# First four blocks' tap sums as diagonal matmuls, and another order of the first blocks

## The chip, the cores and the metric

The kernel runs on one core of one Trainium2 chip. A run's time is device microseconds of that core for one execution. Three runs of the kernel before gave 2386.4, 2385.7 and 2384.95 us, median 2385.7 us.

## The reference

`x` is 4 sequences of 4096 tokens with 192 channels. Each channel is first filtered along the tokens: seven taps, the softmax of a row of `weight` (8 rows, one for each 24 channels), zeros before the start. Then come two layers, the first with weights `moe_w_in`, `moe_w_out`, the second with `moe2_w_in`, `moe2_w_out`; these four are float64.

```
w = exp(weight - max); w = w / (sum(w) + 1e-09)
out = np.einsum('hk,bskhg->bshg', w, x_unf)      # 7 taps
h = x @ w_in                                     # [16384, 192] @ [192, 2048]
g = h * np.cos(h); x = g @ w_out                 # layer 1
h = np.maximum(x @ w_in, 0.0); out = h * h @ w_out   # layer 2
```

## The kernel before

**Tiling.** Channels lie on partitions, tokens on the free axis. The 16384 tokens make 32 blocks `n` of `T` = 512, the 2048 hidden units 16 chunks `c` of 128. An item is (layer `l`, block `n`, chunk `c`), with `l` = 0 for the first layer, 1 for the second. An item has products into `h` (the input side, "IN") and, after its elementwise chain, products into the two accumulators `o` of its block ("OUT"). Every float32 operand of TensorE is split into a rounded part and a rest, and three of the four part products are taken. All matmuls are 64 rows deep; a matmul on the lower 64 rows of the array and one on the upper 64 run as a pair. A step of the plan (a slot) takes IN of two items (18 matmuls) and OUT of two items (20): 19 pairs.

**The chain of an item.** Layer 0: `k` (L591, ScalarE), `f` (L603, VectorE), `sin` (L610, ScalarE), `g` (L617, VectorE), `hi` (L643, ScalarE), `lo` (L648, VectorE). Layer 1: `relu` (L627), `sq` (L636) and `hi`, all ScalarE, then `lo`. For some items of block 1 `lo` may go to GpSimd: 16 do. A bank of `h` is free again after `g` (layer 0) or `relu` (layer 1); there are four banks, two for a slot.

**Before the first layer.** For each block and each of two halves of its channels, `conv` loads `x`, makes the seven taps on VectorE (L375 once, L378 six times), and splits the sum into `xs` (L393, L397).

**Between the layers.** When a block's OUT is done, `ends` takes the sums out (L669, L679), adds the two halves (L698, L699, L723) and splits them into a new `xs` for layer 1 (L710, L715, L729, L734). There are four sets of `xs`.

**Weights.** `prep` loads a float64 weight unit (two chunks, seven DMAs on SyncE, L252 to L259), and makes float32 hi and lo parts of it: VectorE L270, L288, L302, L311, L326, L337 to L341, ScalarE L278, L332. There are 8 units for each layer.

**Two streams.** The items form two streams, `xs` and `ys`: the first holds (0,0), (0,2), (0,3) ... (0,31), (1,31), the second (0,1), (1,0), (1,1) ... (1,30), written (layer, block). A slot mostly takes one item of each. OUT follows IN by 3 slots in the first stream and 2 in the second (`LAGS`). An item that OUT takes alone ("single") is five matmuls in each of two turns, since both turns write the same banks.

**Order.** `Order.run` is a list scheduler with fixed costs: it writes every engine's instructions in one order, each with a due time from `start_of(slot)`. On the chip each engine goes through its list in that order and waits at the head.

Of the kernel before, what the change touches and what calls it, by code (L numbers as in the profile page):

```python
# [27 lines left out]
LEAD = 4  # L28
EARLY = 3
LAGS = (3, 2)  # L30
BUFS = {"raw": 2, "s": 2, "m": 2, "x": 3, "t": 12, "g": 11, "h": 4, "o": 4, "xs": 4}


PAIR, DRAIN, WAY = 233, 170, 90

# [11 lines left out]


def pool(n):
    return 200 + n * 2.4  # L50
# [17 lines left out]
class Order:  # L68
# [14 lines left out]
    def run(self):  # L83
        for s in self.steps:
            s.left = len(s.after)
            for a in s.after:
                a.next.append(s)
        ready = {}
        for s in self.steps:
            if not s.left:  # L90
                self.open(ready, s)
        clock = {}
        done = 0
        while done < len(self.steps):
            best = None
            for e, todo in ready.items():
                now = clock.get(e, 0.0)
                pick = None
                for s in todo:
                    if s.end is not None:  # L100
                        continue
                    at = max(now, s.ready)
                    for kind, n in s.takes:
                        have = self.free[kind]
                        if len(have) < n:
                            break
# [40 lines left out]
def tile_kernel(  # L147
# [10 lines left out]
    engines = {"V": V, "A": A, "G": G}  # L158
# [76 lines left out]
    OX = (HI + U - R, 0)  # L235
# [5 lines left out]
    tiles("m", [P, U], I32)  # L241

    def prep(l, u, due):
# [16 lines left out]

        a = order.add("load" + name, {"S": 400}, load, takes=(("raw", 1),), due=due - 12000, way=5000)
# [80 lines left out]

        return order.add("l" + name, {"V": two(U) + 300}, low, (h,), frees=((d, "m"),), due=due - 1500)


    tiles("x", [P, T + PAD], F32)
# [11 lines left out]
    def conv(n, due):  # L358

        own = order.add(f"x1.{n}", {"N": 0}, lambda s, e: None, takes=(("xs", 1),), due=due - 20000, way=0)  # L360
        last = []
        for j in (0, 1):
            d = due - (1 - j) * 6500

            def load(s, e, j=j):
                nc.sync.dma_start(s.got["x"][0], xp[:, n, j])

            a = order.add(f"x{n}.{j}", {"S": 100}, load, (own,), (("x", 1),), due=d - 12000, way=2500)
            y = b = None
            for k in range(K):  # L370

                def tap(s, e, a=a, y=y, k=k, j=j):
# [11 lines left out]
                    (a, taps) if k == 0 else (b,),  # L384
# [14 lines left out]
            b = order.add(f"xh{n}.{j}", {"A": act(T)} if n < EARLY else {"V": one(T)}, high, (b,), due=d - 1400)  # L399
# [3 lines left out]
        split[0, n] = own, last  # L403

# [113 lines left out]
    first = [(0, 0)] + [(0, n) for n in range(2, NB)] + [(1, NB - 1)]  # L518
    other = [(0, 1)] + [(1, n) for n in range(NB - 1)]
# [3 lines left out]

    slots = []
    x = y = 0
    late = len(xs) - NC
    pend = ([], [])
    while x < len(xs) or y < len(ys) or pend[0] or pend[1]:
        s = len(slots)
        ins = ()  # L530
        if x < LEAD:
            ins = (0, xs[x]), (0, xs[x + 1])
            x += 2
        elif x == late and y < late + LEAD:
            ins = (1, ys[y]), (1, ys[y + 1])
            y += 2
        elif x == late and pend[0]:
            pass
        elif x < len(xs) and y < len(ys):
            ins = (0, xs[x]), (1, ys[y])  # L540
            x, y = x + 1, y + 1
        elif x < len(xs):
            ins = (0, xs[x]), (0, xs[x + 1])
            x += 2
        for k, it in ins:
            pend[k].append(it)
            it.slot = s
        outs = []
# [3 lines left out]
        extra = []  # L552
        while pend[0] and pend[0][0].slot + LAGS[0] < s:
            extra.append(pend[0].pop(0))
        while pend[1] and pend[1][0].slot + LAGS[1] < s:
            extra.append(pend[1].pop(0))
        slots.append((tuple(it for _, it in ins), tuple(outs), tuple(extra)))

# [13 lines left out]
    for (l, u), s in preps.items():  # L572
        weights[l, u] = prep(l, u, start_of(s))
    for (l, n), s in blocks.items():
        if l == 0:
            conv(n, start_of(s))

    def chain(it):
# [44 lines left out]
        else:  # L623
# [23 lines left out]
            {"V": 685, "G": pool(T)} if it.slot < 18 and it.n == 1 else {"V": 685},  # L647
            lambda s, e: engines[e].tensor_tensor(  # L648
# [8 lines left out]
    def ends(it, done):  # L657
# [36 lines left out]
        if l == 0:  # L694
# [45 lines left out]
            if 0 < n < NB - 2:  # L740

                split[0, n + 2][0].after.append(own)
        else:
# [3 lines left out]
                {"S": 100},  # L747
# [21 lines left out]
                {"S": 100},  # L769
# [86 lines left out]
    for s, (ins, outs, extra) in enumerate(slots):  # L856
        for turn in (0, 1):
# [54 lines left out]
```

## Time and profile before

| what | value |
|---|---|
| span of the profiled execution | 2385.6 us |
| time of the profiled execution | 2387.46 us |
| median of three runs | 2385.7 us |
| TensorE busy, matmuls | 2312.1 us (97%), 19456 |
| VectorE busy | 1843.3 us (77%) |
| ScalarE busy | 1911.7 us (80%) |
| GpSimd busy | 30.0 us (1%) |
| mean granted TensorE clock | 0.991 |

The busy time of TensorE counts a matmul from start to modelled end, and two halves overlap, so how far TensorE is from being full is read from the number of matmuls that start in a stretch, not from the 97%.

### The profile page before, as it was taken

Reading aid. Unit: us, or ns where it says so; the run is one execution under the profiler, and the core shown is the slowest. Engines: PE = TensorE matmul, PEld = TensorE weight load, DVE = VectorE, ACT = ScalarE, POOL = GpSimd, SP = SyncE. Lnnn points to the kernel's source line nnn. Section 1 sums busy time; section 2 is a strip of 40 time slices with the busy share of each in tenths; the row PEclk is TensorE's granted clock in tenths of the full one; section 3 lists DMA queues with packets and bytes.
Section 4 is the critical chain, followed back from the end, with each engine's and each line's share of the span. In section 5 each row is a group of like instructions: output and inputs, shape, how many; then the busy total and the mean of one; then the engine's idle time right before and its main releaser. Section 6 shows DMA issues by size and latency. Waiting matters only on the chain.

```text
span 2385.6 us, 46741 instructions
## 1 busy us (share of the span) xinstructions
PE 2312.1 (97%) x19456; PEld 2253.4 (94%) x19456; DVE 1843.3 (77%) x3001; ACT 1911.7 (80%) x3278; POOL 30.0 (1%) x22
## 2 busy tenths in 40 slices
PE   3879999999999999999999999999999999999999
PEld 2668999999999999999999999999999999999988
DVE  8999788777888777788777788877788877778643
ACT  3677888888888888888888888888888888888865
POOL 0220000000000000000000000000000000000000
PEclk9989999999999999999999999999999999999999
DMA  3121000000000000000000000000000000000000
GB/s 106 54 59 40 17 17 17 17 6 12 17 17 17 17 12 6 17 17 17 17 13 5 17 17 17 17 17 3 15 17 17 17 17 8 10 17 8 8 8 14
DMA packets 30820, 45.14 MB, mean 19 GB/s; under 512 B 3984, under 2 KB 12176, under 8 KB 30608
## 3 DMA queue, kind: packets, MB, share of 16 engines
q1 hardware_dynamic: 30608, 42.16, 6.0%
q8 instruction: 152, 2.49, 0.4%
q14 instruction: 60, 0.49, 0.1%
HBM read 29.56 MB, written 12.58 MB: 18 GB/s over the span
## 4 chain that ended last, share of the span: by engine, by line
PE 93%; DVE 5%; SPq 1%; ACT 0%; issue 0%; DMA 0%; POOL 0%; DVEq 0%; ACTq 0%; POOLq 0%
PE o L411 49%; PE h L411 44%; DVE t L378 1%; DVE t L603 1%; DVE t L617 1%; DVE g L648 0%; DVE m L302 0%; DMA raw<-in_w_dram 0%; DVE s L311 0%; SPq L259 0%; DVE wt L337 0%; DVE m L326 0%; DVE s L270 0%; ACT t L591 0%; DVE m L288 0%
## 5 line engine op out<-in xcount | busy, mean ns | idle before, releaser
L411 PE MATMUL o<-g,wt 64*128 64x512 f32 x10240 | 1514.6, 394 | 5.5 <-DVE g L648 2.5
L411 PE MATMUL h<-xs,wt 64*128 64x512 f32 x9216 | 1400.1, 396 | 62.9 <-ACT xs L393 27.5
L411 PEld LDWEIGHTS o<-g,wt 64*128 64x128 f32 x10240 | 1224.5, 185 | 38.4 <-PE o L411 9.3
L411 PEld LDWEIGHTS h<-xs,wt 64*128 64x128 f32 x9216 | 1161.7, 186 | 88.2 <-ACT xs L393 28.0
L648 DVE TENSOR_TENSOR g<-t,g 128x512 fp32r<-128x512 f32 x1008 | 689.0, 684 | 57.1 <-PE o L411 28.2
L643 ACT CAST g<-t 128x512 fp32r<-128x512 f32 x1024 | 625.7, 614 | 116.7 <-DVE t L617 115.5
L603 DVE TENSOR_TENSOR t<-h,t 128x512 f32<-128x512 f32 x512 | 351.3, 687 | 340.8 <-ACT t L591 340.6
L591 ACT ACTIVATE t<-h,quarter 128x512 int32<-128x512 f32 x512 | 350.6, 688 | 238.0 <-PE h L411 237.8
L617 DVE TENSOR_TENSOR t<-t,h 128x512 f32<-128x512 f32 x512 | 348.9, 683 | 116.4 <-ACT t L610 112.8
L610 ACT ACTIVATE t<-t,right 128x512 f32<-128x512 f32 x512 | 364.5, 714 | 27.3 <-DVE t L603 26.4
L636 ACT ACTIVATE t<-t 128x512 f32<-128x512 f32 x512 | 323.3, 635 | 10.3
L627 ACT ACTIVATE t<-h 128x512 f32<-128x512 f32 x512 | 300.4, 590 | 27.3 <-PE h L411 27.3
L378 DVE SCALAR_TENSOR_TENSOR t<-x,wtap,t 128x512 f32<-128x512 f32 x384 | 287.3, 750 | 1.0
L679 DVE TENSOR_SCALAR t<-o 128x512 f32<-128x512 f32 x64 | 43.9, 686 | 14.3 <-PE o L411 13.2
L669 ACT ACTIVATE t<-o 128x512 f32<-128x512 f32 x64 | 38.4, 599 | 8.6 <-PE o L411 8.6
L397 DVE TENSOR_TENSOR xs<-t,xs 128x512 fp32r<-128x512 f32 x64 | 43.4, 680 | 0.0
L648 POOL TENSOR_TENSOR g<-t,g 128x512 fp32r<-128x512 f32 x16 | 29.6, 1853 | 133.6 <-ACT g L643 127.9
L375 DVE TENSOR_SCALAR t<-x,wtap 128x512 f32<-128x512 f32 x64 | 30.5, 479 | 0.0
L393 DVE CAST xs<-t 128x512 fp32r<-128x512 f32 x58 | 24.0, 414 | 0.0
L278 ACT ACTIVATE s<-s 128x768 int32<-128x768 int32 x16 | 13.5, 842 | 12.9 <-DVE s L270 12.8
L715 DVE TENSOR_TENSOR xs<-t,xs 128x512 fp32r<-128x512 f32 x32 | 22.1, 691 | 1.0
L762 DVE TENSOR_TENSOR t<-t,t 64x512 f32<-64x512 f32 x32 | 21.6, 676 | 0.8 <-ACT t L757 0.7
(43 smaller groups left out, 248.6 us busy)
## 6 DMA issues: line engine op xcount, KB each, us to landing
x<-in_xp_dram SPq DMA_DIRECT2D x64, 259.0 KB, 2.8
raw<-in_w_dram SPq DMA_DIRECT2D x16, 512.0 KB, 3.6
out_dram<-t SPq DMA_DIRECT2D x32, 256.0 KB, 2.0
out_dram<-t SPq DMA_DIRECT2D x32, 128.0 KB, 2.2
raw<-in_w_dram SPq DMA_DIRECT2D x32, 64.0 KB, 3.3
raw<-in_w_dram SPq DMA_DIRECT2D x64, 32.0 KB, 2.5
w_sm<-in_wrep_dram SPq DMA_DIRECT2D x1, 7.0 KB, 1.7
```

Source lines behind the costliest of these rows:

```text
L378: V.scalar_tensor_tensor(out=t, in0=xk, scalar=wk, in1=t, op0=ALU.mult, op1=ALU.add)
L397: V.tensor_tensor(out=lo, in0=y.got["t"][0], in1=f32(h), op=ALU.subtract)
L411: return nc.tensor.matmul(bank, w[k, o : o + P], x[k], start=st, stop=sp)
L591: lambda s, e: A.activation(s.got["t"][0].bitcast(I32), h(), AF.Identity, bias=quarter),
L603: lambda s, e: V.tensor_tensor(out=t(), in0=h(), in1=t().bitcast(I32), op=ALU.subtract),
L610: lambda s, e: A.activation(t(), t(), AF.Sin, scale=2.0 * math.pi, bias=right),
L617: lambda s, e: V.tensor_tensor(out=s.got["t"][0], in0=t(), in1=h(), op=ALU.mult),
L627: lambda s, e: A.activation(s.got["t"][0], h(), AF.Relu),
L636: lambda s, e: A.activation(a.got["t"][0], a.got["t"][0], AF.Square),
L643: "hi" + i, {"A": 620}, lambda s, e: A.copy(s.got["g"][0], d.got["t"][0]), (d,), (("g", 1),), due=late - 1500
L648: lambda s, e: engines[e].tensor_tensor(out=s.got["g"][0], in0=d.got["t"][0], in1=f32(it.hi.got["g"][0]), op=ALU.subtract),
L679: V.tensor_scalar(s.got["t"][0], b(), sc, None, op0=ALU.mult)
```

## The change

- Blocks 0 to 3 have their taps on TensorE: `diagonals` makes, for each tap and channel half, a 128x128 diagonal matrix of the tap's weight (a hi part on ScalarE, L468, a lo part on VectorE, L471) from a unit matrix that GpSimd writes at the start (L448, L449). `spread` splits `x` (L429 ScalarE, L437 VectorE), `spread_products` adds two turns of 42 matmuls for a block, and `sums` splits the result out of PSUM (L484, L488). The diagonals and the split `x` lie in the end of the second layer's weight tile, whose late units wait for block 3's products.
- The streams are (0,0), (1,0), (0,2), (0,4) ... and (0,1), (1,1), (0,3), (1,2) ..., and a list `plan` gives the slots; the first stream runs 6 items ahead instead of 4. A plain number in the plan lets a stream's pending OUT run empty.
- `lo` is on VectorE alone. A weight unit takes four DMAs instead of seven. The first four `x` loads are issued by ScalarE. `Order.run` may take a step that can start up to `PATIENCE` later if it is due earlier. `x` has 4 buffers (3), `t` 11 (12).

```diff
-LEAD = 4
-EARLY = 3
+LEAD = 6
+ON_PE = 4
+EARLY = 4
...
+PATIENCE = 250
...
-            {"V": 685, "G": pool(T)} if it.slot < 18 and it.n == 1 else {"V": 685},
+            {"V": 685},
...
+            if n < ON_PE:
+                last += spread(n, j, a, d)
+                continue
...
+    spread_at = {0: (0, 0), 1: (2, 2), 2: (6, 6), 3: (10, 10)}
...
+        def part(j):
+            h, lo = (z.got["xr"][0] for z in spreads[n, j])
+            bank = banks[n][j].got["h"][0]
+            todo = []
+            for k in range(K):
+                todo += [(bank, diag[:, j, k, s], 0, x[:, k : k + T]) for s, x in ((0, h), (0, lo), (1, h))]
+            return todo
...
+        p = product(f"CV{turn}", 21, write, after, (("h", 2),) if turn == 0 else (), frees)
...
-    first = [(0, 0)] + [(0, n) for n in range(2, NB)] + [(1, NB - 1)]
-    other = [(0, 1)] + [(1, n) for n in range(NB - 1)]
+    first = [(0, 0), (1, 0), (0, 2)] + [(0, n) for n in range(4, NB)] + [(1, NB - 1)]
+    other = [(0, 1), (1, 1), (0, 3)] + [(1, n) for n in range(2, NB - 1)]
...
+    plan = [(0, 0)] * (LEAD // 2) + [(0, 1)] * (NC - LEAD) + [(1, 1)] * (LEAD // 2) + [0]
+    plan += [(0, 0)] * (LEAD // 2) + [1] + [(0, 1)] * (late - NC - LEAD) + [(1, 1)] * LEAD + [0]
+    plan += [(0, 1)] * (NC - LEAD) + [(0, 0)] * (LEAD // 2) + [0, 1]
```

On VectorE, before, this stands between the first two weight units and the first split of block 0 (`t` is a tap sum, `xs` its split):

```order
L302 SCALAR_TENSOR_TENSOR m1_73<-raw1_69,m1_73 128x768
L375 TENSOR_SCALAR t0_77<-x0_74,wtap_65 128x512
L375 TENSOR_SCALAR t1_78<-x1_75,wtap_65 128x512
L378 SCALAR_TENSOR_TENSOR t0_77<-x0_74,wtap_65,t0_77 128x512
L378 SCALAR_TENSOR_TENSOR t1_78<-x1_75,wtap_65,t1_78 128x512
...
L375 TENSOR_SCALAR t2_79<-x2_76,wtap_65 128x512
L397 TENSOR_TENSOR xs01_109<-t0_77,xs00_108 128x512
L397 TENSOR_TENSOR xs03_111<-t1_78,xs02_110 128x512
```

In the changed kernel VectorE begins, behind the softmax (`wtap`), like this (`wt2_67` holds the split `x` and the diagonals):

```order
L456 CAST taph_125<-wtap_65 128x14
L460 TENSOR_TENSOR tapl_126<-wtap_65,taph_125 128x14
L437 TENSOR_TENSOR wt2_67<-x0_74,wt2_67 128x518
L437 TENSOR_TENSOR wt2_67<-x1_75,wt2_67 128x518
L471 TENSOR_SCALAR wt2_67<-ident_124,tapl_126 128x128
...
L265 TENSOR_SCALAR s0_70<-raw0_68 128x768
L283 TENSOR_SCALAR m0_72<-raw0_68 128x768
```

The taps are gone, and the 14 small diagonals, which wait for GpSimd's unit matrix `ident`, stand ahead of the first weight unit.

On ScalarE, at the place where block 0's first-layer sums come out (`o0` and, after the change, `o1`), before:

```order
L591 ACTIVATE t3_80<-h3_103,quarter_61 128x512
L669 ACTIVATE t0_77<-o0_104 128x512
L610 ACTIVATE t1_78<-t1_78,right_62 128x512
L698 COPY t7_84<-t6_83 64x512
L699 COPY t7_84<-t6_83 64x512
L710 CAST xs30_120<-t0_77 128x512
```

and in the changed kernel:

```order
L786 ACTIVATE t0_78<-o0_104 128x512
L794 ACTIVATE t10_88<-o1_105 128x512
L815 COPY t3_81<-t10_88 64x512
L816 COPY t3_81<-t10_88 64x512
L827 CAST xs00_108<-t0_78 128x512
L760 CAST g6_95<-t7_85 128x512
L327 CAST wt2_67<-m1_73 128x768
L760 CAST g1_90<-t6_84 128x512
L846 CAST xs02_110<-t10_88 128x512
L273 ACTIVATE s0_70<-s0_70 128x768
L744 ACTIVATE t5_83<-h0_100 128x512
```

Before, first-layer work of other blocks (L591, L610) stands around it; now the next elementwise work after it, L744, is that of the second layer of the same block.

## Rows read from the trace of the kernel before

**Rows 1.** The page: its head.
```profile
span 2385.6 us, 46741 instructions
```
**Rows 2.** Stretches of TensorE: busy us (matmuls), granted clock, DMA share, GB/s.
```profile
0.00:100.00 100.00, 54.23 (x337) 0.97 0.29 87
100.00:200.00 100.00, 85.11 (x630) 0.90 0.21 61
200.00:300.00 100.00, 95.95 (x783) 0.97 0.06 16
...
1000.00:1500.00 500.00, 500.00 (x4289) 1.00 0.05 14
...
2000.00:2300.00 300.00, 298.28 (x2555) 1.00 0.03 10
2300.00:2386.00 86.00, 78.49 (x592) 0.94 0.05 15
...
160.00:164.00 4.00, 4.00 (x22) 0.50 0.00 0
```
**Rows 3.** Who TensorE waited for, 0 to 300 us: total us, times, longest.
```profile
PE h L411 <- ACT xs L393: 27.5, 2, 24.9
PE h L411 <- DVE t L617: 21.4, 12, 8.7
```
**Rows 4.** Stretches: PE, PEld, DVE, ACT, POOL busy us (instructions), clock, DMA, GB/s.
```profile
60.00:70.00 10.00, 9.85 (x73) 7.29 (x73) 10.00 (x15) 6.68 (x11) 2.14 (x1) 0.89 0.18 56
...
140.00:150.00 10.00, 9.58 (x77) 7.66 (x73) 9.72 (x16) 8.29 (x15) 3.85 (x3) 1.00 0.22 74
```
**Rows 5.** The instructions in order of time, 0 to 60 us: start, us, instruction.
```profile
2.46 0.17 DVE L186 TENSOR_REDUCE mx_sm<-w_sm 128x2 f32<-128x14 f32 x1 [2.46 <-DMA w_sm<-in_wrep_dram]
...
16.85 8.03 DVE L378 SCALAR_TENSOR_TENSOR t<-x,wtap,t 128x512 f32<-128x512 f32 x12
...
25.19 1.28 DVE L397 TENSOR_TENSOR xs<-t,xs 128x512 fp32r<-128x512 f32 x2
...
45.59 7.22 PE L411 MATMUL h<-xs,wt 64*128 64x512 f32 x30 [8.66 <-DVE t L617]
...
58.00 1.36 POOL L648 TENSOR_TENSOR g<-t,g 128x512 fp32r<-128x512 f32 x1 [57.14 <-ACT g L643]
```
**Rows 6.** VectorE by line, 57 to 172 us (GpSimd at work): count | busy us, mean ns.
```profile
L617 DVE TENSOR_TENSOR t<-t,h 128x512 f32<-128x512 f32 x32 | 21.1, 675 | 0.0
...
L378 DVE SCALAR_TENSOR_TENSOR t<-x,wtap,t 128x512 f32<-128x512 f32 x12 | 11.9, 991 | 0.0
L302 DVE SCALAR_TENSOR_TENSOR m<-raw,m 128x768 f32<-128x768 uint32 x8 | 10.9, 1360 | 0.0
L270 DVE TENSOR_SCALAR s<-raw 128x768 int32<-128x768 int32 x8 | 8.3, 1035 | 0.0
```
**Rows 7.** The same lines, 172 to 230 us (GpSimd has no work).
```profile
L378 DVE SCALAR_TENSOR_TENSOR t<-x,wtap,t 128x512 f32<-128x512 f32 x12 | 9.0, 748 | 0.0
...
L302 DVE SCALAR_TENSOR_TENSOR m<-raw,m 128x768 f32<-128x768 uint32 x5 | 4.8, 953 | 0.0
...
L270 DVE TENSOR_SCALAR s<-raw 128x768 int32<-128x768 int32 x4 | 2.2, 556 | 0.0
```
**Rows 8.** The page's groups: GpSimd's share of `lo`, and the first tap.
```profile
L648 POOL TENSOR_TENSOR g<-t,g 128x512 fp32r<-128x512 f32 x16 | 29.6, 1853 | 133.6 <-ACT g L643 127.9
L375 DVE TENSOR_SCALAR t<-x,wtap 128x512 f32<-128x512 f32 x64 | 30.5, 479 | 0.0
```
**Rows 9.** TensorE's instructions in order of time near the end.
```profile
2296.37 1.46 PE L411 MATMUL o<-g,wt 64*128 64x512 f32 x10
...
2302.53 1.22 PE L411 MATMUL h<-xs,wt 64*128 64x512 f32 x4 [0.41 <-DVE xs L734]
...
2309.51 1.57 PE L411 MATMUL h<-xs,wt 64*128 64x512 f32 x11
...
2314.91 1.33 PE L411 MATMUL h<-xs,wt 64*128 64x512 f32 x10
...
2367.84 12.61 PE L411 MATMUL o<-g,wt 64*128 64x512 f32 x70
```

More of the change, by code (lines that the diff above doesn't have):

```diff
@@ L1 @@
-import heapq
 import math
@@ L241, in tile_kernel @@
     tiles("m", [P, U], I32)
+    late_writes = {}
     def prep(l, u, due):
@@ new lines, in tile_kernel, with spread @@
+    spreads = {}
+    def spread(n, j, a, due):
+        h = order.add(
+            f"xrh{n}.{j}",
+            {"A": act(T)},
+            lambda s, e: A.copy(s.got["xr"][0], a.got["x"][0]),
+            (a,),
+            (("xr", 1),),
+            due=due - 3000,
+        )
+        lo = order.add(
+            f"xrl{n}.{j}",
+            {"V": two(T)},
+            lambda s, e: V.tensor_tensor(
+                out=s.got["xr"][0], in0=a.got["x"][0], in1=f32(h.got["xr"][0]), op=ALU.subtract
+            ),
+            (h,),
+            (("xr", 1),),
+            ((a, "x"),),
+            due=due - 2000,
+        )
+        spreads[n, j] = h, lo
+        return []
@@ new lines, in tile_kernel, with diagonals, high, low @@
+    G.memset(ident, 1.0)
+    G.affine_select(
+        out=ident, in_=ident, pattern=[[-1, P]], compare_op=ALU.is_equal, fill=0.0, base=0, channel_multiplier=1
+    )
+    def diagonals():
+        done = []
+        a = order.add("taph", {"V": 200}, lambda s, e: V.tensor_copy(taph, wtap), (taps,), due=-40000)
+        b = order.add(
+            "tapl",
+            {"V": 200},
+            lambda s, e: V.tensor_tensor(out=tapl, in0=wtap, in1=f32(taph), op=ALU.subtract),
+            (a,),
+            due=-40000,
+        )
+        for k in range(K):
+            for j in (0, 1):
+                def high(s, e, k=k, j=j):
+                    A.activation(diag[:, j, k, 0], ident, AF.Copy, scale=f32(taph)[:, j, k : k + 1])
+                def low(s, e, k=k, j=j):
+                    V.tensor_scalar(diag[:, j, k, 1], ident, tapl[:, j, k : k + 1], None, op0=ALU.mult)
+                done.append(order.add(f"dh{j}.{k}", {"A": act(P)}, high, (a,), due=-30000 + k))
+                done.append(order.add(f"dl{j}.{k}", {"V": one(P)}, low, (b,), due=-30000 + k))
+        return done
@@ new lines, in sums, with high, low @@
+    def sums(n, s):
+        own = split[0, n][0]
+        for j in (0, 1):
+            bank = banks[n][j]
+            def high(s, e, j=j, bank=bank):
+                A.copy(own.got["xs"][0][2 * j], bank.got["h"][0])
+            def low(s, e, j=j, bank=bank):
+                h, lo = own.got["xs"][0][2 * j : 2 * j + 2]
+                V.tensor_tensor(out=lo, in0=bank.got["h"][0], in1=f32(h), op=ALU.subtract)
+            due = start_of(spread_at[n][1])
+            a = order.add(f"xh{n}.{j}", {"A": 605}, high, (s, own), due=due - 1500)
+            b = order.add(f"xl{n}.{j}", {"V": 690}, low, (a,), frees=((bank, "h"),), due=due - 700)
+            split[0, n][1].extend([a, b])
@@ L551, in tile_kernel @@
                 outs.append(pend[k].pop(0))
[L552 to L556, printed above, removed]
-        slots.append((tuple(it for _, it in ins), tuple(outs), tuple(extra)))
+        for k in (0, 1):
+            while pend[k] and pend[k][0].slot + LAGS[k] < s:
+                extra.append(pend[k].pop(0))
+        slots.append((tuple(it for _, it in ins), tuple(outs), tuple(extra)))
+    for step in plan:
+        if step in (0, 1):
+            while pend[step]:
+                slot(())
+        else:
+            slot([(k, next(todo[k])) for k in step])
+    assert not any(pend) and not any(list(z) for z in todo)
     SLOT = 19 * PAIR
@@ L576, in tile_kernel @@
             conv(n, start_of(s))
+    diagonal = diagonals()
+    for (l, u), s in preps.items():
+        weights[l, u] = prep(l, u, start_of(s))
     def chain(it):
@@ L740, in ends @@
             if 0 < n < NB - 2:
-                split[0, n + 2][0].after.append(own)
+                m = n + 2 if n > 2 else 4 if n == 1 else None
+                if m:
+                    split[0, m][0].after.append(own)
         else:
@@ L856, in tile_kernel @@
     for s, (ins, outs, extra) in enumerate(slots):
+        for n, at in spread_at.items():
+            for turn in (0, 1):
+                if at[turn] == s:
+                    p = spread_products(n, turn)
+                    if n == ON_PE - 1:
+                        for u in range(SPACE // WC, NC // 2):
+                            for z in late_writes[u]:
+                                z.after.append(p)
         for turn in (0, 1):
```

112 lines of the change are left out of this document (61 added, 51 removed).

## The prediction

> **What bounds the kernel now.** I read the stretches of TensorE first. In the middle nothing is lost: 4289 matmuls begin in 500 us, one each 0.1166 us, and a slot of 38 takes 4.43 us [rows 2]. At that pace the 19456 matmuls need 2268.6 us; the span is 2385.6 us [rows 1], so 117.0 us are lost. They lie at the two ends. In the first 300 us 1750 matmuls begin, worth 204.0 us: 96.0 lost. In the last 386 us 3147 begin, worth 366.9 us: 18.7 lost (the span ends at 2385.6) [rows 2]. The other 2.3 us are rounding over the middle. So a change to the first blocks can win at most the 96 us and some of the 18.7.
>
> Who is behind the 96 us is read from the waits: TensorE waits 27.5 us for the first split of block 0 and 21.4 us, twelve times, for `g`, which frees a bank [rows 3]; both come behind VectorE's work. VectorE is full there, 10.00 of 10 us, and 9.72 later, while ScalarE has 6.7 to 8.3 [rows 4]. A count checks it. One 512-wide VectorE instruction follows another after 0.60 us (two take 1.28, the mean of one is 0.68), one tap after 0.67 (twelve in 8.03) [rows 5]; an instruction thus begins 0.08 us before the end of the one ahead. By that and the clean means [rows 7, 8] a weight unit costs VectorE 4.56 us (2 x 0.47, 3 x 0.87, and about 1.0 for the three rests, estimated by their widths). Ahead of the 1136th matmul (about slot 30) the order has on VectorE: softmax 4.2 us, 8 first taps 3.2, 48 taps 32.2, 149 other 512-wide instructions 89.4, four cheaper ones 1.9, weight units 71: 202 us. TensorE has 1135 matmuls, 132.4 us: VectorE is 70 us behind. With the first 8 us, in which it mostly waits for loads, and the stretch below, VectorE gets there at 220 us. TensorE gets there at about 221: 967 matmuls begin before 200 us and 7.8 a microsecond after that [rows 2]. So up to there VectorE sets the pace, and then TensorE does.
>
> **The stretch.** While GpSimd works, three VectorE lines are longer than after it: L378 991 ns against 748 (x12), L302 1360 against 953 (x8), L270 1035 against 556 (x8) [rows 6, 7]: 2.9 + 3.3 + 3.8 = 10.0 us. L617, whose second operand is in PSUM, stays at 675 [rows 6]. GpSimd's 16 subtractions take 29.6 us [rows 8] and spare VectorE 16 x 0.60 = 9.6 us: they give back nothing. The Trainium skill, "SBUF — State Buffer", section "Who interferes with whom", has the reason: VectorE and GpSimd share a port pair, held by one of them for a whole instruction, and a VectorE instruction with two SBUF inputs or in a two-port mode waits. The trace agrees, line by line as above. Without that rule 10 us of the old loss would belong to something that may still be there, and the sum below would be 2379; by the rule it stays as it is.
>
> **What the change costs and gives.**
>
> *TensorE.* 4 blocks x 2 turns x 42 = 336 matmuls more: 19792 x 0.1166 = 2307.7 us, 39.2 more than before. This is certain, and it is paid in full wherever TensorE sets the pace.
>
> *VectorE.* The 56 tap instructions of blocks 0 to 3 go (35.4 us). In come 8 splits of `x` (4.9), 14 small diagonals (128 wide; between 0.13, a quarter of the wide one's 0.47, and 0.40 each: I take 0.14, 2.0 us; at most 5.6) and GpSimd's 16 `lo` (9.6); the stretch goes (10.0). The new order matters more: where block 1's second layer begins (slot 20, matmul 1008), 32 first-layer items have been asked for, where matmul 1136 before had 48 behind it, block 3's taps among the rest. VectorE has ahead of it 120 512-wide instructions (72.6 us), 12 units and a bit (55), softmax 4.4, diagonals 2.0: 134 us; TensorE has 1007 x 0.1166 = 117.4. It is 17 us behind instead of 70.
>
> *The start, step by step, as loss on TensorE.* (a) VectorE's first work is at 2.46 us [rows 5]; 20 softmax steps (4.2), two splits (1.2) and a diagonal put the first matmul at about 9. (b) The first long run before took 7.22 us for 30 matmuls [rows 5], 3.7 more than at full pace; the diagonal products open the kernel and pay it. (c) By slot 3 the order has 37.5 us of VectorE work against 23.8 us of TensorE; from 2.5 us on, with 1 us of its own waits, that is 17.2 us lost, (a) and (b) within it. (d) In slots 3 to 16 VectorE, with two first-layer chains a slot and a unit in most, has just as much to do as TensorE (92 us each between slots 2 and 16, by the order), so neither can hide the other's waits. Between nothing and the 1.8 us a time of before (21.4 / 12 [rows 3]) I take 0.5 us for each of 14 slots: 7. (e) Block 0's second layer begins in the slot right after its last OUT. Then sums out, swap, add and split stand between two matmul groups. Near the end the kernel before has just that: the last `o` ends at 2297.8, the last late group begins at 2302.5 [rows 9], 4.7 us. With another unit and two `hi` now in ScalarE's list there, I take 6, plus 2 for the clock: after such a pause TensorE had a granted 0.50, the 1.2 GHz level, for 4 us [rows 2]. 8. (f) Block 1 has one slot of 18 matmuls (2.1 us) as cover: 4 + 2 = 6. (g) The slots at these seams take 12 items alone. Near the end a slot with two of them took 5.40 us (2309.51 to 2314.91 [rows 9]), 0.49 more for each: 5.9. Sum 17.2 + 7 + 8 + 6 + 5.9 = 44.1 against 96.0.
>
> *The end.* The first stream now runs 6 items ahead, so the last block has two slots between its last OUT and its second layer instead of none. The slot there took from 2297.8 to 2309.5, 11.7 us against 5.4 for the next [rows 9]: 6.3 go. Two more slots with two items alone cost 2.0, two more items alone in the last run of 70 `o` about 1.0. 18.7 - 6.3 + 3.0 = 15.4.
>
> *Nothing, or nearly.* Fewer load issues: VectorE waits for weights only at the start, and SyncE issues far ahead later. The second layer's late units wait for block 3's products in slot 10, before they are needed in slot 20 and after. Slots 36 to 51 have two first-layer chains: 6 x 0.60 = 3.6 us of VectorE in a slot of 4.43, so I count nothing; the price if this fails is a rival.
>
> Total: 2307.7 + 44.1 + 15.4 + 2.3 = **2369.5 us**. The same sum for before gives its span, 2385.6; the median of the runs is 0.1 above that, the profiled execution's own time 1.9 above. I forecast 2369.
>
> **Rivals.**
>
> 1. *Better.* VectorE's lead is enough: (d) nothing, (e) and (f) at the 4.7 us seen and no fall of the clock: 17.2 + 4.7 + 2.6 + 5.9 = 30.4, so 2356. For it: VectorE's backlog in the order is 14 us at slot 3 and about 9 from slot 5 on. Against: TensorE's waits before, and the clock in [rows 2].
> 2. *No change.* (d) at the 1.8 us of before: 25 instead of 7, 2387. For it: four banks, and all three engines close to full. Against: those 1.8 us came with a VectorE that was 35 to 50 us behind.
> 3. *Slower: the bank wait of two first-layer chains.* In a slot `k`, `f`, `sin`, `g` of both items must be done before IN of the slot after next. If that costs 1.8 us in slots 3 to 16 and again in 36 to 51, it is 54 us instead of 7: 2416. It decides from 0.77 us a slot over 30 slots (23 us), where the gain is gone. For it: before, TensorE's twelve waits for `g` [rows 3] all lie where slots hold two such chains. Against: in slots 36 to 51 no weights are made, and VectorE has 0.8 us of 4.43 to spare.
> 4. *The unit matrix is late.* VectorE's diagonals wait for GpSimd and everything stands behind them. All the trace shows is that GpSimd's first large work began at 58.00, when its input came [rows 5]: it was ready at some time before. Ready by 8 us it costs nothing, at 24 us the gain is gone, at 57 it is 2418. A GpSimd instruction takes 1.4 to 1.9 us [rows 5, 8], so I take nothing.
>
> **Chances.** Forecast (2357 to 2381) 0.58, better 0.16, no change 0.12, bank wait 0.10, late matrix 0.04. A measurement tells about 0.2%, 4.8 us, from no change: faster means under 2380.9, slower over 2390.5. Nearly all of the first two cases is faster: 0.73; same 0.13, slower 0.14. The range 2350 to 2394 leaves out a little of the better case and most of the slower ones.
>
> **What would show it.** In the changed profile: 19792 matmuls and the same pitch in the middle; about 44 us lost in the first 300 us and 15 in the last 386; a first matmul near 9 us; one pause of some 6 us near 130 to 145 us behind the sum of block 0 and a smaller one some 15 us later; VectorE at 750 ns a tap and 953 ns for the weight line at all times; no pause near 2300. A first matmul after 15 us, waits for `g` of over 0.8 us in most slots of two first-layer chains, or losses between 200 and 300 us would make the forecast wrong.

## The result and the profile after

The changed kernel takes 2362.46 us (median, 2361.62 to 2362.76, 4 runs); the kernel before, on the same chip, 2386.05 (2384.95 to 2388.38, 4 runs). The ratio is 0.9899, 95% interval [0.9882, 0.9916]: 23.6 us faster. The forecast was 2369, 17 us faster; the range held the time. The profiled execution took 2362.59, its span is 2360.7.

The stretches of TensorE (busy us, matmuls, granted clock, DMA share, GB/s) answer to [rows 2]:

```profile
0.00:100.00 100.00, 86.78 (x658) 0.98 0.34 101
100.00:200.00 100.00, 94.62 (x751) 0.98 0.19 54
200.00:300.00 100.00, 99.89 (x857) 1.00 0.06 20
...
1000.00:1500.00 500.00, 500.00 (x4289) 1.00 0.05 14
2000.00:2300.00 300.00, 299.43 (x2534) 1.00 0.04 11
2300.00:2361.00 61.00, 54.84 (x433) 0.99 0.05 14
```

The pitch is the same, 0.1166 us, so the 19792 matmuls are worth 2307.7 us and 53.0 us of the span are lost. In the first 300 us 2266 begin, worth 264.2: 35.8 lost, 96.0 before. From 2000 us on 2967 begin, worth 346.0 of 360.7: 14.7 lost, 18.7 before. The other 2.5 are put down to the middle. So the start gave back 60.2 us and the end 4.0; the new matmuls took 39.2.

These counts, like those of the prediction, are a little high. A stretch counts every matmul that runs in it, so those under way at a border are counted on both sides. In one stretch of 300 us, first the kernel before, then the changed one:

```profile
0.00:300.00 300.00, 235.29 (x1743) 0.94 0.19 55
0.00:300.00 300.00, 281.28 (x2260) 0.99 0.20 58
```

The prediction has 1750 for the first, and 2266 stands above for the second. Counted by their starts the pitch is 0.1167 us, and in the changed kernel 36.3 us are lost at the start, 15.4 at the end and nothing in the middle: the 2.3 of the prediction and the 2.5 here are this count and not time. What the start and the end gave back changes by less than 0.5 us.

Who TensorE waits for, 0 to 300 us (total us, times, longest), in place of [rows 3], the four longest:

```profile
PE h L531 <- ACT wt L468: 8.8, 1, 8.8
PE h L531 <- ACT xs L827: 3.4, 2, 2.7
PE h L531 <- DVE t L734: 2.7, 2, 2.5
PE h L531 <- ACT xs L846: 0.8, 1, 0.8
```

L531 issues every matmul (L411 before). L468 makes the upper halves of the diagonals, L734 is `g` (L617 before), L827 and L846 are the splits that open the second layer. The two great waits of before, 27.5 and 21.4 us, are gone.

TensorE's instructions in order of time: the start, the seam where block 0's second layer begins (132 us), that of block 1 (150 us), and the end:

```profile
8.76 13.30 PE L531 MATMUL h<-wt 64*128 64x512 f32 x84 [8.76 <-ACT wt L468]
22.74 0.50 PE L531 MATMUL h<-xs,wt 64*128 64x512 f32 x2 [0.68 <-ACT xs L484]
23.47 4.88 PE L531 MATMUL h<-xs,wt 64*128 64x512 f32 x34 [0.22 <-DVE xs L488]
30.81 12.47 PE L531 MATMUL h<-wt 64*128 64x512 f32 x84 [2.46 <-DVE t L734]
43.12 3.98 PE L531 MATMUL h<-xs,wt 64*128 64x512 f32 x30
...
125.16 4.31 PE L531 MATMUL o<-g,wt 64*128 64x512 f32 x30
132.16 0.50 PE L531 MATMUL h<-xs,wt 64*128 64x512 f32 x2 [2.69 <-ACT xs L827]
132.89 0.74 PE L531 MATMUL h<-xs,wt 64*128 64x512 f32 x4 [0.23 <-DVE xs L832]
134.46 1.95 PE L531 MATMUL h<-xs,wt 64*128 64x512 f32 x6 [0.83 <-ACT xs L846]
...
146.29 2.82 PE L531 MATMUL h<-xs,wt 64*128 64x512 f32 x18
149.79 0.50 PE L531 MATMUL h<-xs,wt 64*128 64x512 f32 x2 [0.67 <-ACT xs L827]
...
2277.45 1.56 PE L531 MATMUL h<-xs,wt 64*128 64x512 f32 x11
...
2282.83 1.56 PE L531 MATMUL h<-xs,wt 64*128 64x512 f32 x11
```

The loss is read at marks: the time less the matmuls that stand ahead of it in the program, times 0.1166. Slot 3 begins at 43.12 with 204 ahead (23.8 us): 19.3 lost. The OUT of slot 16 ends at 129.2 with 904 (105.4): 23.8. Slot 19 begins at 146.29 with 980 (114.3): 32.0. At 300 us it is 35.8. Near the end slot follows slot every 5.38 us and nothing pauses where [rows 9] had 11.7.

VectorE by line, 57 to 172 us (count | busy us, mean ns), the first weight line of [rows 6], L302 there:

```profile
L297 DVE SCALAR_TENSOR_TENSOR m<-raw,m 128x768 f32<-128x768 uint32 x10 | 9.6, 957 | 0.3
```

It is at 957 ns where it was 1360; GpSimd has no work there now.

### The profile page after: what moved, and what is told of

Same layout as the page of the kernel before. It is cut to its first block, busy times and chain, and to the rows that moved or that the text cites. A ratio compares the mean times of both kernels' runs of the same rounds, so it can differ in the third digit from the quotient of the medians.

```text
span 2360.7 us, 47177 instructions
## 1 busy us (share of the span) xinstructions
PE 2335.5 (99%) x19792; PEld 2276.7 (96%) x19792; DVE 1845.3 (78%) x2980; ACT 1943.2 (82%) x3305; POOL 0.8 (0%) x8
## 4 chain that ended last, share of the span: by engine, by line
PE 98%; DVE 1%; ACT 1%; DMA 0%; issue 0%; ACTq 0%; DVEq 0%
PE o L531 51%; PE h L531 47%; DMA raw<-in_w_dram 0%; DVE t L734 0%; DMA x<-in_xp_dram 0%; DVE t L720 0%; ACT t L786 0%; DVE wt L437 0%; ACT t L816 0%; ACT t L708 0%; ACT t L815 0%; DVE m L321 0%; ACT wt L327 0%; DVE xs L488 0%; ACT g L760 0%
## 5 line engine op out<-in xcount | busy, mean ns | idle before, releaser
L531 PE MATMUL o<-g,wt 64*128 64x512 f32 x10240 | 1517.0, 393 | 2.1
L531 PE MATMUL h<-xs,wt 64*128 64x512 f32 x9216 | 1389.5, 392 | 6.3 <-ACT xs L827 3.4
L531 PEld LDWEIGHTS o<-g,wt 64*128 64x128 f32 x10240 | 1223.8, 184 | 37.2 <-PE o L531 17.7
L531 PEld LDWEIGHTS h<-xs,wt 64*128 64x128 f32 x9216 | 1161.9, 184 | 23.0 <-ACT xs L827 4.2
L765 DVE TENSOR_TENSOR g<-t,g 128x512 fp32r<-128x512 f32 x1024 | 696.6, 686 | 155.0 <-ACT g L760 105.7
L760 ACT CAST g<-t 128x512 fp32r<-128x512 f32 x1024 | 594.5, 617 | 33.5 <-DVE t L734 22.2
L734 DVE TENSOR_TENSOR t<-t,h 128x512 f32<-128x512 f32 x512 | 348.1, 684 | 49.5 <-ACT t L727 49.1
L744 ACT ACTIVATE t<-h 128x512 f32<-128x512 f32 x512 | 299.5, 591 | 30.7 <-PE h L531 30.7
L753 ACT ACTIVATE t<-t 128x512 f32<-128x512 f32 x512 | 317.6, 624 | 4.0
L382 DVE SCALAR_TENSOR_TENSOR t<-x,wtap,t 128x512 f32<-128x512 f32 x336 | 251.0, 747 | 2.1
L531 PE MATMUL h<-wt 64*128 64x512 f32 x336 | 46.4, 425 | 11.6 <-ACT wt L468 8.8
L531 PEld LDWEIGHTS h<-wt 64*128 64x128 f32 x336 | 38.9, 204 | 18.2 <-ACT wt L468 8.8
L786 ACT ACTIVATE t<-o 128x512 f32<-128x512 f32 x64 | 38.3, 599 | 10.7 <-PE o L531 10.7
L401 DVE TENSOR_TENSOR xs<-t,xs 128x512 fp32r<-128x512 f32 x56 | 38.4, 685 | 0.1
L840 DVE TENSOR_TENSOR t<-t,t 128x512 f32<-128x512 f32 x32 | 22.1, 691 | 13.6 <-ACT t L816 13.5
L327 ACT CAST wt<-m 128x768 fp32r<-128x768 f32 x16 | 13.3, 833 | 12.7 <-DVE m L321 12.7
```

The source lines that it names most:

```text
L382: V.scalar_tensor_tensor(out=t, in0=xk, scalar=wk, in1=t, op0=ALU.mult, op1=ALU.add)
L401: V.tensor_tensor(out=lo, in0=y.got["t"][0], in1=f32(h), op=ALU.subtract)
L531: return nc.tensor.matmul(bank, w[k, o : o + P], x[k], start=st, stop=sp)
L734: lambda s, e: V.tensor_tensor(out=s.got["t"][0], in0=t(), in1=h(), op=ALU.mult),
L744: lambda s, e: A.activation(s.got["t"][0], h(), AF.Relu),
L753: lambda s, e: A.activation(a.got["t"][0], a.got["t"][0], AF.Square),
```

## The experiments

Twelve kernels were made from the two. Each ratio is to the kernel before timed beside it, whose median was 2387.05 (e1, e2, e3, e5), 2386.69 (e4, e8, e9, e10) or 2386.10 us (e11 to e14).

### Two ways to the same end: the order and the tap sums

**e1**: the changed kernel, all tap sums on VectorE.

```
-ON_PE = 4
+ON_PE = 0
-    spread_at = {0: (0, 0), 1: (2, 2), 2: (6, 6), 3: (10, 10)}
+    spread_at = {}
...
-    diagonal = diagonals()
```

The lines left out give the first splits of blocks 0 to 2 to ScalarE, as before, and let the first tap wait for the softmax.

> The changed kernel with the taps of blocks 0 to 3 on VectorE again; order of blocks, GpSimd without work, load issues and the end as changed. Theory (VectorE's work ahead of a TensorE group sets the start): by the order VectorE is at most 63 us behind, at block 0's second layer, so with 9 us of start and some 6 us of seams and single items 78 us are lost in the first 300 us; 2268.6 + 78 + 15 + 2.3 = 2364, between 2360 and 2374. Rival (the taps on TensorE are the whole gain): as the kernel before, 2386.

**e2**: the changed kernel with the order of blocks of before; tap sums of four blocks stay on TensorE.

```
-LEAD = 6
+LEAD = 4
-    first = [(0, 0), (1, 0), (0, 2)] + [(0, n) for n in range(4, NB)] + [(1, NB - 1)]
+    first = [(0, 0)] + [(0, n) for n in range(2, NB)] + [(1, NB - 1)]
...
```

> The changed kernel with the streams of before, (0,0) (0,2) (0,3) ... and (0,1) (1,0) (1,1) ..., and 4 items of lead: only the taps on TensorE, the loads and GpSimd stay changed. Theory: VectorE is at most 14 us behind by the order, no group stands directly behind the sum it needs, so about 19 us up to slot 3, 5 of waits and 2 of single items are lost at the start, 26 instead of 36; the end loses 18.7 as before: 2307.7 + 26 + 18.7 + 2.3 = 2355, between 2350 and 2362. Rival (the blocks side by side carry the gain): 2375 or more, and losses between 100 and 300 us.

**e10**: both edits. What is left is the rest of the change.

> The changed kernel with the order of blocks of before (side-by-side order gone, four lead slots, as in e2) and with all tap sums on VectorE (no diagonals, as in e1): what is left of the change is no GpSimd subtraction, the joined loads, the list scheduler's new choice and the new rings. It fills the fourth corner of the two-by-two with e1 (new order, taps on VectorE, 2364.95), e2 (old order, taps on TensorE, 2358.97) and the changed kernel (both, 2362.46). Theory A (order and taps are two ways to the same end, each takes VectorE's work of the first 200 us out of TensorE's way, so the second adds almost nothing): this kernel is far behind all three, near the kernel before without GpSimd (2379.9): 2379 (2374 to 2386). Rival B (the other edits carry the gain, and neither order nor taps is worth much): 2363 (2360 to 2368). Rival C (without either, the new list rule and rings hurt): 2390 or more. First stretch of 100 us under A: some 345 matmuls, second 680, third 770; under B over 640 and 780.

Measured, in us:

| | taps on VectorE | taps of four blocks on TensorE |
|---|---|---|
| order of before | e10 2381.89 (2373.94 to 2384.94), 0.9971 [0.9959, 0.9982] | e2 2358.97 (2357.5 to 2359.79), 0.9882 [0.9868, 0.9895] |
| new order | e1 2364.95 (2363.55 to 2365.28), 0.9905 [0.989, 0.992] | changed 2362.46 |

All three came as the first theory had them. The order alone wins 16.9 us, the taps alone 22.9, the two together 19.4: they take the same loss away, and with the taps on TensorE the new order costs 3.5. (The intervals of those two ratios overlap. In the traces the changed kernel loses 5.1 us more than e2 in the first 300 us and 2.4 less from 2000 us on.) (Four of e10's ten runs lie near 2374, six at 2382 to 2385; measured from the four, order and taps are worth 9 and 15, which changes neither statement.) The other parts of the change, GpSimd's share among them, are worth the 4.8 us of e10. That is less than e3 below finds for GpSimd's share alone (7.2), but e10's two groups of times lie further apart than the difference. The starts differ more than the times do. First e1, then e2:

```profile
0.00:100.00 100.00, 57.79 (x351) 0.97 0.31 93
100.00:200.00 100.00, 92.52 (x697) 0.93 0.22 61
200.00:300.00 100.00, 100.00 (x855) 1.00 0.07 20
```

```profile
0.00:100.00 100.00, 85.67 (x657) 0.98 0.34 101
100.00:200.00 100.00, 95.64 (x797) 0.98 0.19 54
200.00:300.00 100.00, 99.64 (x857) 1.00 0.05 15
```

By these counts e1 has 1903 matmuls in 300 us and the changed kernel 2266, 363 more. But 336 of those are the tap sums themselves: only 27, 3.1 us, are headway.

### GpSimd's share given back

**e3**: the kernel before, with GpSimd's 16 `lo` on VectorE.

```
-            {"V": 685, "G": pool(T)} if it.slot < 18 and it.n == 1 else {"V": 685},
+            {"V": 685},
```

> The kernel before with the 16 subtractions of block 1 on VectorE instead of GpSimd. Theory: VectorE gets 16 x 0.60 = 9.6 us more and loses about 10 us of stretch: 2386, between 2381 and 2391. Rival (work taken off VectorE is a gain): 2396. Rival (the whole 29.6 us of GpSimd is lost on VectorE): 2366.

2379.88 (2378.54 to 2381.45, 7 runs), 0.9971 [0.9961, 0.9982]: 7.2 us faster, and outside what every theory said. The lines of VectorE, 57 to 172 us, in e3:

```profile
L648 DVE TENSOR_TENSOR g<-t,g 128x512 fp32r<-128x512 f32 x40 | 27.0, 682 | 0.2 <-ACT g L643 0.2
...
L378 DVE SCALAR_TENSOR_TENSOR t<-x,wtap,t 128x512 f32<-128x512 f32 x12 | 8.9, 742 | 0.0
L302 DVE SCALAR_TENSOR_TENSOR m<-raw,m 128x768 f32<-128x768 uint32 x8 | 7.6, 948 | 0.0
L311 DVE SCALAR_TENSOR_TENSOR s<-raw,s 128x768 int32<-128x768 int32 x7 | 6.6, 948 | 0.0
...
L270 DVE TENSOR_SCALAR s<-raw 128x768 int32<-128x768 int32 x8 | 4.4, 550 | 0.0
L340 DVE TENSOR_TENSOR wt<-m,wt 128x64 fp32r<-128x64 f32 x8 | 1.7, 217 | 0.0
```

And lines of the kernel before in the same stretch, beside those of [rows 6] (L288, not shown, goes from 687 to 551 ns):

```profile
L648 DVE TENSOR_TENSOR g<-t,g 128x512 fp32r<-128x512 f32 x21 | 15.3, 732 | 0.1
...
L311 DVE SCALAR_TENSOR_TENSOR s<-raw,s 128x768 int32<-128x768 int32 x7 | 7.7, 1099 | 0.0
...
L340 DVE TENSOR_TENSOR wt<-m,wt 128x64 fp32r<-128x64 f32 x8 | 2.8, 350 | 0.0
```

The prediction counted three stretched lines, 10.0 us. By these means there are seven: L378 3.0, L302 3.3, L270 3.9, L311, L288 and L340 1.1 each, L648 1.0 (21 x 0.05), in all 14.5. The means hide how it comes about. In order of time, in the kernel before:

```profile
58.00 1.36 POOL L648 TENSOR_TENSOR g<-t,g 128x512 fp32r<-128x512 f32 x1 [57.14 <-ACT g L643]
58.14 1.30 DVE L340 TENSOR_TENSOR wt<-m,wt 128x64 fp32r<-128x64 f32 x1
```

L340 starts while GpSimd subtracts and takes 1.30 us where it takes 0.22 otherwise. In the whole trace 14 VectorE instructions are longer than their clean mean, one beside each of 14 of GpSimd's 16 subtractions, by 0.77 to 1.09 us each, 14.5 in all. Which of the seven lines is hit depends on what VectorE has in hand just then; the others that overlap a subtraction have their clean length. Less the 9.6 us that GpSimd spared, VectorE lost 4.9 by its help. This agrees with the rule that the prediction took from the Trainium skill ("SBUF — State Buffer", section "Who interferes with whom"): a VectorE instruction waits while GpSimd's runs, and in e3, where GpSimd is idle, the lines have their clean means. What failed was the list of lines. The other 2.3 of the 7.2 us are not explained; that an item waits 0.6 us for `lo` in place of 1.85 [rows 8] may be part of it, which was not tried by itself.

### The end alone

**e4**: the kernel before, with more cover ahead of the last block.

```
-        elif x == late and y < late + LEAD:
+        elif x == late and y < late + LEAD + 4:
```

> The kernel before, with one edit: at the end four more pairs of the second stream's chains stand ahead of the last block, as the changed kernel has them in another form; the start is as before. Theory A (the wait of 6.3 us ahead of the last block's chains is end-bound and goes, four to eight single slots cost some 0.5 us each): 2383 (2380.5 to 2384.5), a gain of 2 to 5. Rival B (the pause is hidden by what follows or the singles eat it): 2387 (2385 to 2389). In the stretch 2000 to 2300 us TensorE starts 2530 or more matmuls under A.

2384.64 (2383.19 to 2385.35, 11 runs), 0.9990 [0.9981, 0.9999]: 2.1 us faster, just above the first theory's range and below the second's. From 2000 to 2300 us TensorE is busy all the time, with 2575 matmuls, 20 more than before, so the pause is gone. Of its 6.3 us some 4 are paid back, by the prediction's 0.49 us for each of eight more items alone (a slot with two of them takes 5.40 us here as in [rows 9]). So the sign and the mechanism of the end's term hold, and the gain is small (the interval of the ratio just misses 1).

### The order on VectorE

**e8**: the scheduler's new allowance set to nothing.

```
-PATIENCE = 250
+PATIENCE = 0
```

> The changed kernel, with the list scheduler's new allowance (250 units, within which it takes the step due first and not the one ready first) set to 0, so that the step ready first goes first as in before; nothing else. By sums over the program order (multiplied by durations of the trace) VectorE's work ahead of TensorE's exceeds it by at most 30 us in place of 17. Theory A (VectorE's order is what sets the start's loss): TensorE waits some 10 to 13 us more in the first 150 us: 2374 (2367 to 2380). Rival B (order within a quarter of a microsecond's rank is off the path): 2362.5 (2360 to 2365). Rival C (earlier release helps): under 2359.

2372.22 (2371.78 to 2374.94), 0.9943 [0.9930, 0.9957]: 9.8 us slower than the changed kernel, as the first theory had it. TensorE's first matmul:

```profile
19.46 10.90 PE L531 MATMUL h<-wt 64*128 64x512 f32 x72 [19.46 <-ACT wt L468]
```

It comes 10.7 us later. In the trace steps that are ready sooner and due later, weight units above all, stand between those of the softmax and ahead of the diagonals. This line of the diff, which the prediction did not price, is worth as much as TensorE pays for a whole block's tap sums (84 x 0.1166 = 9.8 us).

### How many blocks on TensorE

**e5**, **e14**: the changed kernel with the tap sums of two and of three blocks on TensorE. **e9**, **e11**: e5 with eight and with four lead items instead of six.

```
-ON_PE = 4
+ON_PE = 2
-    spread_at = {0: (0, 0), 1: (2, 2), 2: (6, 6), 3: (10, 10)}
+    spread_at = {0: (0, 0), 1: (2, 2)}
```

This is e5. e14 has `ON_PE = 3` and keeps block 2 in `spread_at`; e9 and e11 add `LEAD = 8` and `LEAD = 4`.

> The changed kernel with only blocks 0 and 1 on TensorE, the taps of 2 and 3 on VectorE. Theory: TensorE saves 168 matmuls, 19.6 us; by the order VectorE is at most 31 us behind instead of 17, so 14 us come back at the start: about 6 us faster than the change, 2356, between 2349 and 2362. Rival (VectorE has no room for any taps in the first 300 us, all 17.5 us come back and more in waits): 2363 to 2375.

> The changed kernel with tap sums of three blocks (0, 1, 2) on TensorE. Four take 2362.5, two 2351.7, none 2365.0. Theory A (each block adds 84 matmuls, 9.8 us, in full, and takes its vector work away from a sum that counts only as far as it runs ahead of TensorE's; the lead falls from 30.7 to 23.4 from two to three blocks, worked out from the program's order and durations of the trace): 2357 (2354.5 to 2359.5). Rival B (the seam of the second pair of blocks costs the same with one block as with two on VectorE; the best is at three): 2350 or less. Rival C (block 2 and 3 must go the same way since they go side by side): 2361 or more.

> The changed kernel with tap sums of blocks 0 and 1 alone on TensorE (as in e5, 2351.7), and eight lead slots at each seam instead of six. Theory A (what is left at the seams, 6.2 and 1.8 us in the changed kernel, is cover that lacks at the tail of block 0 and 1): the waits at the seams go, four more single slots cost 0.5 us each: 2348 (2344 to 2352). Rival B (the seams' losses are the clock and the first cold slots, not cover; more singles cost): 2353.5 (2352 to 2356). Under A the stretch 100 to 200 holds over 760 matmuls in place of 736.

> The changed kernel with tap sums of blocks 0 and 1 alone on TensorE, as in e5 (2351.7), and four lead slots at each seam instead of six; e9 had eight and took 2355.9. Theory A (each single slot costs its half microsecond and the cover of four is enough, because what TensorE waits for at the start is VectorE's sum of work and not the order of the chains): from 32 single slots' worth less, another 2 to 4 us gained: 2349 (2347 to 2351). Rival B (the seams open again with less cover, as the kernel before waited at its end with four): 2354 to 2360.

| kernel | us | ratio |
|---|---|---|
| no block (e1) | 2364.95 | 0.9905 [0.989, 0.992] |
| two (e5) | 2351.71 (2344.16 to 2353.14) | 0.9845 [0.9831, 0.9859] |
| three (e14) | 2354.72 (2346.87 to 2355.56) | 0.9858 [0.9839, 0.9877] |
| four (changed) | 2362.46 | 0.9899 [0.9882, 0.9916] |
| two, eight lead items (e9) | 2355.88 (2347.35 to 2357.34) | 0.9865 [0.9850, 0.9881] |
| two, four lead items (e11) | 2363.45 (2361.2 to 2365.51) | 0.9904 [0.9889, 0.9919] |

Of these two blocks do best, 10.7 us under the changed kernel and 35.3 under the one before: e5 beats both. Its interval overlaps that of three blocks, so the two are not told apart, and one block was not tried. (e5, e9 and e14 each have one time 6 to 8 us below the next, as e10 has four; medians are used, and the cause is open.) For e9 the second theory was right; for e11 its direction was, and the time is 3.5 above its range; e14 came as its first theory had it. Of the covers tried six does best. Stretches of e11:

```profile
260.00:280.00 20.00, 17.76 (x134) 15.97 (x134) 17.91 (x31) 14.24 (x24) 0.00 (x0) 0.91 0.05 14
280.00:300.00 20.00, 16.90 (x128) 14.87 (x126) 14.17 (x23) 15.65 (x28) 0.00 (x0) 0.91 0.00 1
```

(PE, PEld, VectorE, ScalarE, GpSimd busy us and counts, clock, DMA share, GB/s.) In e5 TensorE is busy for all of both stretches, with 176 and 174 matmuls: 350 against 262, and 88 are worth 10.3 us, where the spans are 9.4 apart. Up to 260 us e11 is ahead by 16 (1845 to 1829). With less cover it is not the first seams that open but a later one. The two long waits of e11 there:

```profile
263.16 0.50 PE L531 MATMUL h<-xs,wt 64*128 64x512 f32 x1 [1.54 <-DVE t L734]
...
286.62 0.50 PE L531 MATMUL h<-xs,wt 64*128 64x512 f32 x2 [2.63 <-ACT xs L827]
```

The first is for a bank; e5 has such a wait too, 0.99 us at 257.62. The second is for the split that opens block 2's second layer, at the 2011th matmul; e5 waits for nothing from 260 to 330 us. After each the granted clock of a stretch of 4 us is at 0.57 or 0.58. From the 1830th matmul to the 2000th e11 loses 5.3 us, from there to the 2100th 5.5; e5 loses nothing in either.

### A warm start for TensorE

**e12**: e5, with matmuls on zeros while TensorE has nothing else to do.

```
+    warm = order.free["g"][-1][2].bitcast(mybir.dt.bfloat16)
+    V.memset(warm[:, 0:T], 0.0)
+    for _ in range(17):
+        nc.tensor.matmul(order.free["h"][-1][2], warm[:, 0:P], warm[:, 0:T], start=True, stop=True)
```

> e5 (tap sums of blocks 0 and 1 on TensorE, 2351.7), with 17 matmuls of 128x128 by 128x512 on zeros at the program's start, while TensorE would wait for its first 8.9 us; their result is written over. It takes away the half clock of the first tap sums (84 matmuls in 13.30 us in the changed kernel, where full clock gives 9.8). Theory A (in the first 100 us VectorE sets the end, so that TensorE's early 3.5 us only turn into later waits): 2351 (2349.5 to 2353). Rival B (TensorE's cold start is on the path in full): 2348 (2346 to 2349). Under both the first 84 real matmuls take about 10 us.

2354.76 (2353.23 to 2356.4), 0.9868 [0.9853, 0.9883]: nothing gained, against the 2348 of the second theory; 1.8 us above the first theory's range. The order of time in e12:

```profile
1.25 5.36 PE L456 MATMUL h<-g 128*128 128x512 bf16 x17 [1.25 <-DVE g L454]
8.95 10.71 PE L536 MATMUL h<-wt 64*128 64x512 f32 x84 [2.34 <-ACT wt L473]
21.86 0.51 PE L536 MATMUL h<-xs,wt 64*128 64x512 f32 x2 [2.20 <-ACT xs L489]
23.71 6.35 PE L536 MATMUL h<-xs,wt 64*128 64x512 f32 x34 [1.34 <-DVE xs L493]
```

In e5 the same runs took 13.41, 0.50 and 4.88 us, with waits of 0.68 and 0.23 between. The first 84 matmuls are 2.7 us shorter, and the next two waits 2.6 us longer. Then, after these pauses, the 34 take 1.5 us more, with a granted 0.50 from 26 to 28 us. So a faster start is waited away, for steps behind VectorE's and ScalarE's work.

### The load issues

**e13**: the changed kernel, a pair of weight columns loaded by seven issues as before, not four (the same bytes).

```
-            nc.sync.dma_start(parts[:, 0 : U // R : U // R - 1], both[:, :, 2 * P : P + D])
+            nc.sync.dma_start(raw[:, 0:R], rows[0:P, 2 * P : P + D])
+            nc.sync.dma_start(raw[:, U - R :], rows[P:, 2 * P : P + D])
...
-                nc.sync.dma_start(parts[half, 9:11], rest)
+                for h in (0, 1):
+                    nc.sync.dma_start(parts[half, 9 + h : 10 + h], rest[:, h : h + 1])
```

> The changed kernel with each pair of weight columns loaded by seven DMA issues as in before, not four; the same bytes to the same places. Theory A (SyncE has time for them, nothing waits for the loads of a pair but the first): 2362.5 (2361 to 2364). Rival B (three issues of some 0.4 us a pair ahead of the x loads and of the first weights push the first tap sums back, or delay later x loads): 2366 to 2370, with the first matmul after 10 us instead of at 8.76.

2362.74 (2361.99 to 2363.1), 0.9901 [0.9886, 0.9916]: no difference, first matmul at 8.74. That part of the change does nothing, as predicted.

## Why the prediction was right, and where its sizes were off

The sum was 2369.5 for a span of 2360.7: 8.8 too much, 8.3 of it in the start.

| step | forecast | measured |
|---|---|---|
| matmuls | 2307.7 | 2307.7 |
| (a) to (c), up to slot 3 | 17.2 | 19.3 |
| (d) slots 3 to 16 | 7 | 2.5 (23.8 - 19.3, less 2.0 for four singles) |
| (e) seam of block 0 | 8 | 6.2 (32.0 - 23.8, less 2.0) |
| (f) seam of block 1 | 6 | 1.8 (35.8 - 32.0, less 2.0); by starts 2.4 |
| (g) twelve singles | 5.9 | 6.0, taken from the end's 0.49 each, not measured here |
| end | 15.4 | 14.7 |
| middle | 2.3 | 2.5; by starts nothing |

**Start, (a) to (c).** The first matmul came at 8.76, forecast 9, though the softmax began at 3.30 and not at 2.46: its input landed after 2.5 us, with four loads of `x` beside it. The first 84 matmuls took 3.5 us over the pace, forecast 3.7. What was missing is a second slow burst: the bank wait of 2.46 us before block 1's diagonals, and after it a granted 0.50, so that its 84 took 2.7 more than the pace.

**(d) was mis-sized most.** VectorE and TensorE had the same work there, and the prediction gave each slot half a microsecond of waits that neither could hide. From 44 to 130 us TensorE waits once, for 0.2 us, so nearly all of the 2.5 that is lost there is not waiting. (The two tap sums in it take 10.3 and 10.2 us for 84 matmuls, 0.9 over the pace; the rest is open.) The bank wait, rival 3, does not come: `g` is waited for 2.7 us in all, and the wait that was read off before (1.8 us each) belonged to a VectorE that was far behind, as the prediction's own word against rival 2 had it.

**(e) and (f).** The path through sum, swap and split was there: 2.69, 0.23 and 0.83 us of waits, and a granted 0.58 from 134 to 136 us. At block 1 it is one wait of 0.67 us and the granted clock stays at 1.00; the 2 us for the clock were not due and the cover was nearly enough.

**What gave the gain.** The prediction said that the new order matters more than the taps. It does not: alone it wins 16.9 us to their 22.9 (e1 and e2, 6.0 apart, were timed beside each other), and beside them it costs 3.5. And GpSimd's help did not "give back nothing": without it the kernel before is 7.2 us faster. This moved no term of the sum, since the new start was counted from VectorE's own list, but 7.2 of the old start's 96.0 us went with GpSimd's help, where the prediction had nothing. The late unit matrix, rival 4, is out: it was ready at 1.43 us.

```profile
1.14 0.29 POOL L449 TENSOR_SCALAR_AFFINE_SELECT ident<-ident 128x128 f32<-128x128 f32 x1
```

**One number would have done better.** The prediction worked out VectorE's lead, the most by which its list, up to what a matmul needs, exceeds TensorE's work ahead of that matmul: 70 before (80 with its stretch), 17 after. It then added local losses slot by slot. Take instead what the kernel before loses beside its lead, 2385.6 - 2268.6 - 80 = 37.0, and keep it: 2307.7 + 17 + 37.0 = 2361.7, where 2360.7 was measured. That it comes so near is partly luck: with the stretch of 14.5 us that e3 shows in place of 10 it would be 2357. The same sums, from each program's order and the durations of [rows 5, 7, 8], for the other kernels:

| kernel | TensorE's work | VectorE's lead | span | rest |
|---|---|---|---|---|
| before (stretch as in e3, 14.5) | 2268.6 | 84.5 | 2385.6 | 32.5 |
| e3, before without GpSimd | 2268.6 | 79.7 | 2379.3 | 31.0 |
| e10, old order, no taps | 2268.6 | 79.7 | 2381.0 | 32.7 |
| e1, new order, no taps | 2268.6 | 63.1 | 2363.6 | 31.9 |
| e5, two blocks | 2288.2 | 30.7 | 2351.4 | 32.5 |
| e9, two, eight lead items | 2288.2 | 32.1 | 2355.5 | 35.2 |
| e11, two, four lead items | 2288.2 | 29.9 | 2360.8 | 42.7 |
| e14, three blocks | 2298.0 | 23.4 | 2352.8 | 31.4 |
| changed, four blocks | 2307.7 | 16.9 | 2360.7 | 36.1 |
| e2, old order, four blocks | 2307.7 | 14.2 | 2357.9 | 36.0 |
| e8, no allowance | 2307.7 | 30.4 | 2373.1 | 35.0 |

The rest is 31 to 36 us in ten of eleven (the exception is e11, with its loss after 260 us). It stands for what the lead leaves out, among it the first 9 us, the slow first matmuls, the singles and the end; it was not taken apart. The spans are of one execution each, and e10, e5, e9 and e14 have others some 8 to 10 us shorter, for which the rest would be smaller by as much. A block's taps on TensorE cost 9.8 us there and take from VectorE's lead 63.1 - 30.7 = 32 for the first two, but only 7.3 and 6.5 for the third and fourth: past two, by this sum, it is a loss. e8 and e14 were forecast by this sum, 2374 and 2357, and took 2372.2 and 2354.7; that it held for the others was seen afterwards, and e11 shows that it is no law. By the same sums e11's lead has its peak not at the first seam alone but again at the seam of block 2's second layer, where the trace has its late wait; the most that VectorE is behind does not say how often TensorE meets it.

## What to carry to other kernels

When a helper engine is behind only at the start, work out its lead over the engine that sets the rest, and weigh a change by what it takes off that lead against what it adds to the busy engine; two edits that cut the same lead do not add up, and the amount moved is best tried in steps (here two or three blocks did better than none or four). Price a helper on a shared port by how often it works, here about 1 us of VectorE for each of 14 of 16 instructions, and not by the mean of the lines that look worst. Local waits read off a kernel that is far behind are no price for one that is level.

## What the hardware showed beside this

The slow first matmuls do not show in the granted clock. TensorE in the changed kernel, two stretches at the start and one after the pause before 30.81 us:

```profile
12.00:14.00 2.00, 2.00 (x12) 1.00 0.00 0
...
18.00:20.00 2.00, 2.00 (x20) 1.00 0.20 54
...
32.00:34.00 2.00, 2.00 (x12) 0.50 0.00 1
```

Twelve in a stretch of 2 us is the pace at a granted 0.50, the 1.2 GHz level, yet the first row says 1.00. The 1.00 is not a reading. The trace's first record of the granted clock is at 14.8 us, and a stretch without a record is printed as full. Up to that record a matmul starts every 0.22 us, and between 18 and 20 us every 0.11. In e12, where 5.36 us of other matmuls stand ahead, the first record is at 4.4 us, and the same stretch holds 20:

```profile
12.00:14.00 2.00, 2.00 (x20) 1.00 0.00 0
```

In e11 it is at 12.0 us, and there too the pace doubles. So the start runs at the lower level, and for it the pace of the matmuls is the better clock. The Trainium skill, "TensorE: Matmul & The Clock Gate", Part 1, says that the lower level is where the engine stands until work releases it; these paces agree. Also, loads of `x` issued from ScalarE at the start took 4.7 us to land (median of 4) where SyncE's 60 took 3.1; the start's other loads ran beside them, so the engine that issued them is not shown to be the cause.
